# Attention order rewritten: single score tiles with short weighted sums, turns in pairs, row sums for three units at once

## Chip, cores, metric

The kernel runs on one core of one Trainium2 chip. The metric is the device time of one execution in microseconds (us), and the median of several runs is compared. The profile is one further execution, taken by the hardware profiler. PE is TensorE (PEld its weight loads), DVE is VectorE, ACT ScalarE, POOL GpSimd, and SP the engine that issues nearly all DMAs (its queue is shown as SPq).

## The reference, cut

```python
# attention with a learned relative bias, B, H, S, D = 8, 8, 576, 64
scores = (1 / sqrt(D)) * q @ k.T
psi_rel = log1p(abs(i - j)); psi_i = log1p(max(i, 1))
bias = relu((psi_rel / psi_i)[..., None] @ w1 + b1) @ w2       # one value per head
attn = softmax(scores + bias)
x = (attn @ v).transpose(0, 2, 1, 3).reshape(B * S, H * D)     # 4608 x 512
# gated experts' shape, without a nonlinearity; d_ff = 1024
h = (x @ moe_w1) * (x @ moe_w2) @ moe_w3
return h @ moe_w_out
```

## The kernel before

It has three stages. A prologue computes the bias of all heads and writes it to DRAM. Then comes attention, and after it the expert part, whose weights are narrowed from wide words and split into two parts so that matmuls can run in a faster format; `moe_w3` is first multiplied with `moe_w_out` ("fold"), then each block of 512 tokens goes through `up` (L566) and `down` (L592).

Attention goes over 32 **units**. A unit is a pair of heads `p` (4) and a batch entry `b` (8), with `p` outermost, and has nine **tiles** of 128 rows of scores by 576 columns: tiles 0 to 7 hold 128 query rows of one head each (odd ones the second head), tile M the last 64 rows of both heads. The letters below are the names of the steps:

- `lk`, `lq`, `lv`, `c0`, `xd`, `rd`: DMAs on SP. `lk` and `lq` load k and q of a unit (576 KB each, two buffers), `lv` loads v four times, once for each 32 partitions (288 KB each, two buffers), `xd` stores the weighted sums `x`, `rd` the reciprocal row sums in twelve small stores, `c0` loads a piece of an expert weight.
- `S` (L233) on PE: the scores of one tile, four matmuls in 64x64 shape, into one of two PSUM buffers. The trace shows each of these four-byte matmuls as two matmuls with a weight load each, so 8 a tile.
- `T` (L248) on DVE: adds the bias, scales, and takes the row extreme; this frees the PSUM buffer.
- `E` (L270) on ACT: the exponential, with the row sum accumulated into a column of `SUMS`.
- `R` (L280) on DVE: turns the tile in blocks of 32x32 (`nc.vector.transpose`) into `PT`, of which there are two.
- `r` (L283) on DVE: adds a small constant to nine row sums, takes reciprocals and turns them; then `rd`.
- `W` (L301) on PE: the weighted sums, in 32x64 shape, over 18 blocks of 32 keys. Each block is 16 matmuls in the trace, so a unit has 288. Before, they come in four parts of 5, 4, 5 and 4 blocks, that is 80, 64, 80 and 64 matmuls. The first needs the turns of all nine tiles, and the PSUM tile `acc` has one buffer.
- `X` (L318) on ACT: copies `acc` to `x`.
- `c1` to `c7`: a piece of an expert weight is narrowed on the side in 24 of the 32 units, with two steps on ACT, a clamp (L134) and two last steps (L151, L152) on POOL and three steps on DVE (L137, L143, L148).

The order on PE, ACT, DVE and POOL is written out by hand. `arrange` (L38) gives each step a planned time within a unit, in us from the unit's start, and an engine; `drive` (L157) sorts all steps by that time and issues them in that order, so the times decide only which step stands before which on its engine. What an engine really waits for are the semaphores of the tiles. SP takes its DMAs in the same order. A later DMA on SP waits behind an earlier one that can't be issued yet. Each DMA also uses one of eight completion semaphores in turn, and waits for the DMA that used the same one before it.

In the middle of a unit PE's order before is, with the units' distance behind the point:

```
PE  S0 W3(-2) S1 S2 S3 W0(-1) S4 S5 W1(-1) S6 S7 W2(-1) SM | S0 W3(-1) ...
DVE R7(-1) c6 T1 r(-1) RM(-1) T2 R0 T3 R1 T4 R2 T5 R3 T6 R4 T7 R5 c4 TM R6 c5 | T0 ...
SP  lk(+1) lq(+1) c0 lv xd(-2) rd(-1)
```

The weights `w1` and `w2` of the experts are narrowed after attention by the same function `narrow` (L110), in `split_w` (L483).

Of the kernel before, what the change touches and what calls it, by code (L numbers as in the profile page):

```python
# [34 lines left out]
PART_AT = 12, 14, 16, 18


def arrange(NU, pieces):  # L38
# [18 lines left out]
    at["c1"] = 5 * L_T + 2.5, "ACT"  # L57
    at["c2"] = 6 * L_T + 2.5, "ACT"
    at["c3"] = 6 * L_T + 2.0, "POOL"
    for n in range(3):  # L60
        at[f"c{4 + n}"] = (7 + n) * L_T + 2.0, "DVE"
    at["c7"] = 9 * L_T + 3.0, "POOL"
    return {(n, u): (u * PERIOD + t + 1.1, e) for u in range(NU) for n, (t, e) in at.items() if n[0] != "c" or u in pieces}


@with_exitstack
def relpos_attention_moe(
# [39 lines left out]
    LEAST = struct.unpack("<f", struct.pack("<I", 0x38000000))[0]  # L107
    MOST = struct.unpack("<f", struct.pack("<I", 0x47EFFFFF))[0]

    def narrow(pool, src, n, x, queue, pieces=1):  # L110

        d = {}

# [17 lines left out]
            nc.scalar.activation(x, d["lo"].bitcast(U32), AF.Copy, scale=2.0 ** -52)  # L131

        def clamp():
            nc.gpsimd.tensor_scalar(d["mag"], d["mag"], LEAST, MOST, op0=ALU.max, op1=ALU.min)  # L134

        def shift():
            nc.vector.tensor_scalar(  # L137
# [140 lines left out]
    SLOT = {t: 4 if t == "M" else int(t) // 2 + 5 * (int(t) % 2) for t in TILES}

    def op_R(u, t):  # L280
        nc.vector.transpose(PT[u % 2][:, SLOT[t]], st[u].pop(("p", t)))  # L281

    def op_r(u, n):  # L283
        p, b = units[u]
        d = st[u]
        if n == "":
            r = SUMS[u % 3]
            nc.vector.tensor_scalar(r[:, 0:9], r[:, 0:9], 1e-9, None, op0=ALU.add)
            nc.vector.reciprocal(r[:, 0:9], r[:, 0:9])
            d["rt"] = sm.tile([P, 32], F32, name="rt")  # L290
            nc.vector.transpose(d["rt"], r)
            return
        rows = r_d[p][:, b * S:(b + 1) * S]
        for a in range(4):
            for h in range(2):
                o = rows[h, 0:512].rearrange("(i a j) -> a i j", a=4, j=32)[a]
                nc.sync.dma_start(o, d["rt"][32 * a + 4 * h:32 * a + 4 * h + 4])
# [1 line left out]
            nc.sync.dma_start(rows[h:h + 1, j:j + 32], d["rt"][32 * a + 8:32 * a + 9])
# [405 lines left out]
```

## Time and profile before

| | us |
|---|---|
| runs: median (lowest, highest) of 3 | 1337.45 (1331.56, 1342.58) |
| profiled execution: its time | 1344.74 |
| profiled execution: span | 1342.9 |
| first score turn `T` of unit 0 starts | 63.3 |
| last `T` of unit 31 starts | 662.6 |
| expert part, bound by PE, from | 805 |

PE is busy 1147.8 us of the span, DVE 709.0, ACT 495.2, POOL 213.8. The page divides the span into 40 slices of 33.6 us: slices 3 to 20 are attention. A row of a timeline has the start, the duration, the engine, the line, the operation, what is written and read, and in brackets how long the engine was idle before it and what ended the wait; "issue" means that nothing in the profile explains it. In tables of windows each engine has its busy time with the number of instructions, and behind them stand the granted clock of TensorE (1.00 is full), the share of time in which DMA engines were busy, and GB/s.

### The profile page before, as it was taken

To read this page: it belongs to the slowest core of one execution; us is meant where nothing else is said; L and a number is where in the kernel's file an instruction comes from. 1 tells how busy PE (TensorE), PEld (TensorE's weight loads), DVE (VectorE), ACT (ScalarE), POOL (GpSimd) and SP (SyncE) were. 2 spreads that over 40 slices of the span, in tenths; PEclk is the share of its full clock that TensorE was granted. 3 is DMA by queue.
4 is the path that set the end of the run, shared out by engine and by line. 5 is a ranking of instruction groups with operands and counts; after the bars stand their busy time and mean duration, and the time that the engine had idled before them with its cause. 6 is when DMAs were issued, how large, how long until landed. Compare 5 with 4: busy or idle time off the path is not lost. (4 is left out here: it accounts for less than half of the span.)

```text
span 1342.9 us, 34477 instructions
## 1 busy us (share of the span) xinstructions
PE 1147.8 (85%) x14720; PEld 825.3 (61%) x14720; DVE 709.0 (53%) x1468; ACT 495.2 (37%) x1071; POOL 213.8 (16%) x169
## 2 busy tenths in 40 slices
PE   8677777776777768767788999999999999999998
PEld 3244444443544444444576868888888888888887
DVE  8597777767787776687757452222222222222211
ACT  6665545444455444454543332121212121212121
POOL 0012210212012220122256660000000000000000
PEclk9888878888888888788889999999999999999999
DMA  8955567556666567566343221110111110200000
GB/s 255 289 154 165 166 181 218 155 152 176 208 186 170 159 195 198 145 185 172 101 127 125 94 79 59 36 64 32 63 32 63 32 63 32 70 25 32 0 32 32
DMA packets 61497, 158.51 MB, mean 118 GB/s; under 512 B 10400, under 2 KB 18720, under 8 KB 57248
## 3 DMA queue, kind: packets, MB, share of 16 engines
q1 hardware_dynamic: 60912, 156.30, 39.6%
q8 instruction: 115, 1.88, 0.6%
q14 instruction: 38, 0.31, 0.1%
q10 hardware_dynamic: 432, 0.02, 0.0%
HBM read 126.36 MB, written 29.92 MB: 116 GB/s over the span
## 5 line engine op out<-in xcount | busy, mean ns | idle before, releaser
L313 PE MATMUL acc<-pt,v 32*64 32x160 f32 (+1 forms) x9216 | 247.7, 338 | 109.1 <-issue 97.9
L275 ACT ACTIVATE pp<-ts,mx 128x576 f32<-128x576 f32 x288 | 223.1, 775 | 289.5 <-DVE mx L254 285.3
L313 PEld LDWEIGHTS acc<-pt,v 32*64 32x64 f32 x9216 | 195.9, 154 | 184.1 <-issue 166.6
L243 PE MATMUL s<-k,q 64*64 64x288 f32 x2304 | 217.4, 480 | 56.4 <-DVE mx L254 39.0
L254 DVE CUSTOM_DVE_ANT_0 ts<-s,nb 128x576 f32<-128x576 f32 x256 | 186.6, 729 | 78.1 <-PE s L243 63.9
L583 DVE TENSOR_TENSOR g<-up,a 128x512 f32<-128x512 f32 x72 | 49.8, 691 | 337.2 <-PE up L575 337.2
L575 PE MATMUL up<-xh,wl 128*128 128x512 f32 x576 | 225.9, 392 | 2.1 <-DVE wl L494 2.1
L575 PE MATMUL up<-xh,wh 128*128 128x512 f32 x576 | 225.8, 392 | 0.2 <-ACT wh L491 0.2
L575 PE MATMUL up<-xl,wh 128*128 128x512 f32 x576 | 225.6, 392 | 0.0
L281 DVE STREAM_TRANSPOSE pt<-pp 128x576 f32<-128x576 f32 x288 | 221.5, 769 | 0.3 <-ACT pp L275 0.3
L600 PE MATMUL o<-w3s,gh 128*128 128x512 f32 x576 | 178.0, 390 | 0.1
L243 PEld LDWEIGHTS s<-k,q 64*64 64x64 f32 x2304 | 78.2, 150 | 156.9 <-DVE mx L254 85.3
L134 POOL TENSOR_SCALAR wmag<-wmag 128x512 f32<-128x512 f32 x40 | 78.7, 1969 | 355.5 <-ACT wmag L128 354.9
L580 ACT COPY a<-up 128x512 f32<-128x512 f32 x72 | 42.2, 586 | 249.5 <-PE up L575 249.5
L575 PEld LDWEIGHTS up<-xh,wl 128*128 128x128 f32 x576 | 108.3, 188 | 26.7 <-DVE wl L494 3.4
L575 PEld LDWEIGHTS up<-xh,wh 128*128 128x128 f32 x576 | 108.5, 188 | 24.4 <-ACT wh L491 1.0
L575 PEld LDWEIGHTS up<-xl,wh 128*128 128x128 f32 x576 | 108.5, 188 | 23.4
L600 PEld LDWEIGHTS o<-w3s,gh 128*128 128x128 f32 x576 | 108.0, 188 | 23.5 <-ACT gh L586 0.8
L586 ACT ACTIVATE gh<-g 128x512 fp32r<-128x512 f32 x72 | 45.5, 632 | 184.3 <-DVE g L583 184.3
L600 PE MATMUL o<-w3s,gl 128*128 128x512 f32 x288 | 112.3, 390 | 0.9 <-DVE gl L589 0.9
L561 POOL TENSOR_SCALAR xh<-xr 128x512 fp32r<-128x512 f32 x36 | 23.5, 652 | 437.1 <-DVE xr L557 430.4
L589 DVE TENSOR_TENSOR gl<-g,gh 128x512 fp32r<-128x512 f32 x72 | 50.8, 705 | 51.5 <-ACT gh L586 51.5
(63 smaller groups left out, 906.2 us busy)
## 6 DMA issues: line engine op xcount, KB each, us to landing
v<-in_v_dram SPq DMA_DIRECT2D x128, 288.0 KB
k<-in_k_dram SPq DMA_DIRECT2D x32, 576.0 KB
q<-in_q_dram SPq DMA_DIRECT2D x32, 576.0 KB
wi<-in_moe_w_dram SPq DMA_DIRECT2D x32, 512.0 KB
nb_d<-bev SPq DMA_DIRECT2D x36, 295.5 KB
nb<-nb_d SPq DMA_DIRECT2D x16, 576.0 KB
x_d<-x SPq DMA_DIRECT2D x32, 288.0 KB
xr<-x_d SPq DMA_DIRECT2D x36, 256.0 KB
```

The lines of the kernel that those rows point to most:

```text
L134: nc.gpsimd.tensor_scalar(d["mag"], d["mag"], LEAST, MOST, op0=ALU.max, op1=ALU.min)
L243: nc.tensor.matmul(s[outs, hf, :HS], d["q"][rows, h * S + q0:h * S + q0 + 64], d["k"][rows, h * S + hf * HS:h * S + (hf + 1) * HS], start= ...
L254: nc.vector.tensor_tensor_reduce(out=halves(ts), in0=d.pop(("s", t))[:, :, :HS], in1=halves(NB[p, t]), op0=ALU.add, op1=ALU.min, scale=-1. ...
L275: nc.scalar.activation(pp, ts, AF.Exp, bias=mx, scale=-1.0, accum_out=SUMS[u % 3][:, col:col + 1])
L281: nc.vector.transpose(PT[u % 2][:, SLOT[t]], st[u].pop(("p", t)))
L313: nc.tensor.matmul(acc[outs, a, c0:c0 + 32 * (t1 - t0)], x[rows, (h * NBK + b) * D:(h * NBK + b + 1) * D], pt_[rows, t0:t1, 32 * b:32 * b ...
L575: nc.tensor.matmul(acc, l[:, cc], r, start=(n == 0), stop=(n == 3 * NC - 1))
L580: nc.scalar.copy(a, ps[0])
L583: nc.vector.tensor_tensor(g, ps[1], a, op=ALU.mult)
L586: nc.scalar.activation(gh, g, AF.Copy)
L589: nc.vector.tensor_tensor(gl, g, f(gh), op=ALU.subtract)
L600: nc.tensor.matmul(d["o", t], l[:, sl], folded[ft][:, r], start=(ft == 0 and n == 0), stop=(ft == NF - 1 and n == 2),)
```

## The change

The order of attention is written anew, in four ways.

- The tiles are taken as 0 2, 1 3, 4 6, 5 7, M. The exponentials of a pair go to two halves of one tile of 1152 columns, and one `R` turns both (M alone). There are three buffers for a pair and one for M where four held a tile each.
- The weighted sums are in eight parts of 3, 2, 2, 2, 3, 2, 2, 2 blocks, that is 48 or 32 matmuls, and each stands behind a single score tile.
- `r` finishes 27 row sums after every third unit; its `rd` then has 36 stores, and 24 after the last two units.
- The buffers of the pieces (`cva`) become two. `narrow` does its clamp on DVE, except for the pieces within attention, which name POOL as before.

By the new times the order in the middle of a unit is:

```
PE  S0 W6(-2) S2 W7(-2) S1 S3 W0(-1) S4 W1(-1) S6 W2(-1) S5 W3(-1) S7 W4(-1) SM W5(-1) | S0 W6(-1) ...
DVE T0 T2 r(-1) RM(-1) T1 T3 R02 T4 T6 R13 c4 T5 T7 R46 c5 TM R57 c6 | T0 ...
SP  lk(+1) lq(+1) c0 lv xd(-2) rd(-1, every third unit)
```

```diff
-L_T = 1.39
+L_T = 1.43
 PERIOD = 9 * L_T
-TILES = "01234567M"
-NPP, NTS = 4, 3
-PARTS = ((0, 5), (5, 9), (9, 14), (14, 18))
-PART_AT = 12, 14, 16, 18
+TILES = "02134657M"
+PAIRS = ("02", "13", "46", "57", "M")
+NPP, NTS = 3, 3
+PARTS = ((0, 3), (3, 5), (5, 7), (7, 9), (9, 12), (12, 14), (14, 16), (16, 18))
...
 def arrange(NU, pieces):
...
     for k, t in enumerate(TILES):
-        a = k * L_T
-        at["S" + t] = a - 1.1, "PE"
-        at["T" + t] = a + 0.9, "DVE"
-        at["E" + t] = a + 1.7, "ACT"
-        at["R" + t] = a + 2 * L_T + 1.6, "DVE"
-    at["r"] = 10 * L_T + 1.55, "DVE"
-    at["rd"] = 10 * L_T + 2.5, "SP"
-    for n, k in enumerate(PART_AT):
-        at[f"W{n}"] = k * L_T - 0.6, "PE"
+        t_of[k] = (k - k % 2) * L_T + 2.0 + 0.66 * (k % 2)
+        at["T" + t] = t_of[k], "DVE"
+        at["E" + t] = t_of[k] + 0.75, "ACT"
+    s_of = {}
+    for k, t in enumerate(TILES):
+        s_of[k] = t_of[k - 2] + 0.7 if k > 1 else t_of[7 + k] - PERIOD + 0.7
+        at["S" + t] = s_of[k], "PE"
+    for n, ts in enumerate(PAIRS[:-1]):
+        at["R" + ts] = (t_of[2 * n + 2] + (1.33 if n < 3 else 0.67)), "DVE"
+    at["RM"] = PERIOD + t_of[0] + 1.33, "DVE"
+    at["r"] = PERIOD + t_of[0] + 1.30, "DVE"
+    at["rd"] = PERIOD + t_of[0] + 2.5, "SP"
+    for n in range(len(PARTS)):
+        u, k = divmod(n + 3, 9)
+        at[f"W{n}"] = (u + 1) * PERIOD + s_of[k] + 0.3, "PE"
...
-    def narrow(pool, src, n, x, queue, pieces=1):
+    def narrow(pool, src, n, x, queue, pieces=1, clamps=nc.vector):
...
-            nc.gpsimd.tensor_scalar(d["mag"], d["mag"], LEAST, MOST, op0=ALU.max, op1=ALU.min)
+            clamps.tensor_scalar(d["mag"], d["mag"], LEAST, MOST, op0=ALU.max, op1=ALU.min)
...
-    cva = ctx.enter_context(tc.tile_pool(name="cva", bufs=1))
+    cva = ctx.enter_context(tc.tile_pool(name="cva", bufs=2))
...
     def op_E(u, t):
         d = st[u]
         ts, mx = d.pop(("t", t))
-        pp = d["p", t] = ppool.tile([P, S], F32, name="pp", bufs=NPP)
-        col = 8 if t == "M" else int(t) // 2 + 4 * (int(t) % 2)
-        nc.scalar.activation(pp, ts, AF.Exp, bias=mx, scale=-1.0, accum_out=SUMS[u % 3][:, col:col + 1])
+        ps = PAIR[t]
+        if ("p", ps) not in d:
+            if t == "M":
+                d["p", ps] = ppool.tile([P, S], F32, name="ppM")
+            else:
+                d["p", ps] = ppool.tile([P, 2 * S], F32, name="pp", bufs=NPP)
+        k = ps.index(t)
+        col = 9 * (u % 3) + (8 if t == "M" else int(t) // 2 + 4 * (int(t) % 2))
+        nc.scalar.activation(
+            d["p", ps][:, k * S:(k + 1) * S], ts, AF.Exp, bias=mx, scale=-1.0,
+            accum_out=SUMS[u // 3 % 2][:, col:col + 1],
+        )
...
-    def op_R(u, t):
-        nc.vector.transpose(PT[u % 2][:, SLOT[t]], st[u].pop(("p", t)))
+    def op_R(u, ts):
+        s0 = SLOT[ts[0]]
+        o = PT[u % 2][:, s0:s0 + len(ts)].rearrange("p t j -> p (t j)")
+        nc.vector.transpose(o, st[u].pop(("p", ts)))
...
     def op_r(u, n):
+        if u % 3 < 2 and u < NU - 1:
+            return
+        if n == "":
+            r = SUMS[u // 3 % 2]
+            nc.vector.tensor_scalar(r[:, 0:27], r[:, 0:27], 1e-9, None, op0=ALU.add)
+            nc.vector.reciprocal(r[:, 0:27], r[:, 0:27])
+            st[u]["rt"] = sm.tile([P, 32], F32, name="rt")
+            nc.vector.transpose(st[u]["rt"], r)
+            return
+        for w in range(u // 3 * 3, u + 1):
+            sums_out(w, st[u]["rt"][:], 9 * (w % 3))
```

More of the change, by code (lines that the diff above doesn't have):

```diff
@@ L27 @@
 AT_W = 3.5, 0.0, 0.5, 1.2, 2.6, 3.8, 5.5, 7.1, 10.0, 10.6
-L_T = 1.39
+L_T = 1.43
 PERIOD = 9 * L_T
-TILES = "01234567M"
-NPP, NTS = 4, 3
-PARTS = ((0, 5), (5, 9), (9, 14), (14, 18))
-PART_AT = 12, 14, 16, 18
+TILES = "02134657M"
+PAIRS = ("02", "13", "46", "57", "M")
+NPP, NTS = 3, 3
+PARTS = ((0, 3), (3, 5), (5, 7), (7, 9), (9, 12), (12, 14), (14, 16), (16, 18))
 def arrange(NU, pieces):
     at = {}
+    t_of = {}
     for k, t in enumerate(TILES):
-        a = k * L_T
-        at["S" + t] = a - 1.1, "PE"
-        at["T" + t] = a + 0.9, "DVE"
-        at["E" + t] = a + 1.7, "ACT"
-        at["R" + t] = a + 2 * L_T + 1.6, "DVE"
-    at["r"] = 10 * L_T + 1.55, "DVE"
-    at["rd"] = 10 * L_T + 2.5, "SP"
-    for n, k in enumerate(PART_AT):
-        at[f"W{n}"] = k * L_T - 0.6, "PE"
-    at["X"] = PART_AT[-1] * L_T + 1.5, "ACT"
+        t_of[k] = (k - k % 2) * L_T + 2.0 + 0.66 * (k % 2)
[13 more added lines that the diff above has]
+        at[f"W{n}"] = (u + 1) * PERIOD + s_of[k] + 0.3, "PE"
+    at["X"] = at["W7"][0] + 0.9, "ACT"
     at["xd"] = at["X"][0] + 0.8, "SP"
@@ L56, in arrange @@
     at["c0"] = 0.2, "SP"
[L57 to L63, printed above, removed]
+    at["c1"] = t_of[1] + 1.6, "ACT"
+    at["c2"] = t_of[3] + 1.6, "ACT"
+    at["c3"] = t_of[2] + 1.0, "POOL"
+    at["c4"] = t_of[4] + 1.34, "DVE"
+    at["c5"] = t_of[6] + 1.34, "DVE"
+    at["c6"] = t_of[8] + 0.68, "DVE"
+    at["c7"] = t_of[8] + 2.0, "POOL"
+    return {(n, u): (u * PERIOD + t + 1.4, e) for u in range(NU) for n, (t, e) in at.items() if n[0] != "c" or u in pieces}
 @with_exitstack
@@ L264, in relpos_attention_moe @@
     SUMS = []
-    for i in range(3):
+    for i in range(2):
         t = att.enter_context(tc.tile_pool(name=f"sums{i}", bufs=1)).tile([P, 32], F32, name=f"sums{i}")
@@ L268, in relpos_attention_moe @@
         SUMS.append(t)
+    PAIR = {t: ts for ts in PAIRS for t in ts}
     def op_E(u, t):
@@ L272, in op_E, with sums_out @@
         ts, mx = d.pop(("t", t))
-        pp = d["p", t] = ppool.tile([P, S], F32, name="pp", bufs=NPP)
-        col = 8 if t == "M" else int(t) // 2 + 4 * (int(t) % 2)
-        nc.scalar.activation(pp, ts, AF.Exp, bias=mx, scale=-1.0, accum_out=SUMS[u % 3][:, col:col + 1])
+        ps = PAIR[t]
[10 more added lines that the diff above has]
+        )
     SLOT = {t: 4 if t == "M" else int(t) // 2 + 5 * (int(t) % 2) for t in TILES}
-    def op_R(u, t):
-        nc.vector.transpose(PT[u % 2][:, SLOT[t]], st[u].pop(("p", t)))
+    def op_R(u, ts):
+        s0 = SLOT[ts[0]]
+        o = PT[u % 2][:, s0:s0 + len(ts)].rearrange("p t j -> p (t j)")
+        nc.vector.transpose(o, st[u].pop(("p", ts)))
     def op_r(u, n):
-        p, b = units[u]
[L285 to L292, printed above, removed]
+        if u % 3 < 2 and u < NU - 1:
[9 more added lines that the diff above has]
+            sums_out(w, st[u]["rt"][:], 9 * (w % 3))
+    def sums_out(u, rt, c0):
+        p, b = units[u]
         rows = r_d[p][:, b * S:(b + 1) * S]
@@ L296, in op_r @@
                 o = rows[h, 0:512].rearrange("(i a j) -> a i j", a=4, j=32)[a]
-                nc.sync.dma_start(o, d["rt"][32 * a + 4 * h:32 * a + 4 * h + 4])
+                nc.sync.dma_start(o, rt[32 * a + c0 + 4 * h:32 * a + c0 + 4 * h + 4])
             h, j = a // 2, 512 + a % 2 * 32
-            nc.sync.dma_start(rows[h:h + 1, j:j + 32], d["rt"][32 * a + 8:32 * a + 9])
+            nc.sync.dma_start(rows[h:h + 1, j:j + 32], rt[32 * a + c0 + 8:32 * a + c0 + 9])
     def op_W(u, n):
@@ L337, in piece_of @@
         if i < NF:
-            return narrow(cva, moe_w_out[i * P:(i + 1) * P, :], DO, wos[i], nc.sync)
+            return narrow(cva, moe_w_out[i * P:(i + 1) * P, :], DO, wos[i], nc.sync, clamps=nc.gpsimd)
         ft, hf = divmod(i - NF, 2)
         cs = slice(hf * 512, (hf + 1) * 512)
-        return narrow(cva, moe_w3[ft * P:(ft + 1) * P, cs], 512, w3s[ft][:, cs], nc.sync)
+        return narrow(cva, moe_w3[ft * P:(ft + 1) * P, cs], 512, w3s[ft][:, cs], nc.sync, clamps=nc.gpsimd)
     pieces = dict(zip([u for u in range(NU) if 0 < u % B < B - 1], (piece_of(i) for i in range(3 * NF))))
```

## The prediction

> **What bounds the kernel now.** I read the windows first, then the timeline of TensorE over one unit, then VectorE, the weight loads and the DMA issues. The window from the first score turn (`op_T`) of unit 3 to the first one of unit 31 holds 28 units; columns are PE, PEld, DVE, ACT, POOL busy with counts, then granted clock, DMA share, GB/s.
>
> ```profile
> 107.12:647.67 540.55, 394.05 (x10084) 240.53 (x10080) 401.06 (x907) 265.12 (x633) 97.98 (x66) 0.85 0.63 176
> ```
>
> 540.55 / 28 = **19.3 us a unit**. PE is busy 14.1 of it, DVE 14.3: no engine is full, so the unit is set by waits. TensorE over a little more than one unit (start, duration, engine, idle before it and its releaser):
>
> ```profile
> 312.88 0.50 PE L313 MATMUL acc<-pt,v 32*64 32x128 f32 x9 [3.18 <-issue]
> 313.31 1.48 PE L243 MATMUL s<-k,q 64*64 64x288 f32 x16
> 314.72 2.94 PE L313 MATMUL acc<-pt,v 32*64 32x160 f32 x80
> 317.59 1.20 PE L243 MATMUL s<-k,q 64*64 64x288 f32 x16
> 318.72 1.37 PE L313 MATMUL acc<-pt,v 32*64 32x160 f32 x64
> 320.02 0.72 PE L243 MATMUL s<-k,q 64*64 64x288 f32 x8
> 321.14 0.71 PE L243 MATMUL s<-k,q 64*64 64x288 f32 x8 [0.41 <-DVE mx L254]
> 322.82 0.71 PE L243 MATMUL s<-k,q 64*64 64x288 f32 x8 [0.96 <-DVE mx L254]
> 324.90 2.98 PE L313 MATMUL acc<-pt,v 32*64 32x160 f32 x80 [1.37 <-issue]
> 327.81 1.20 PE L243 MATMUL s<-k,q 64*64 64x288 f32 x16
> 328.94 1.37 PE L313 MATMUL acc<-pt,v 32*64 32x160 f32 x64
> 330.23 1.23 PE L243 MATMUL s<-k,q 64*64 64x288 f32 x14
> 334.53 1.11 PE L243 MATMUL s<-k,q 64*64 64x288 f32 x2 [3.07 <-issue]
> ```
>
> Twice PE stops for over 3 us in the middle of a run of matmuls that wait for no tile ("issue"), the second time inside one score part (14 + 2). Between the two stops stand 9+16+80+16+64+8+8+8+80+16+64+14 = 383 matmuls. The page says what comes in lumps of that kind:
>
> ```profile
> PE 1147.8 (85%) x14720; PEld 825.3 (61%) x14720; DVE 709.0 (53%) x1468; ACT 495.2 (37%) x1071; POOL 213.8 (16%) x169
> ...
> q8 instruction: 115, 1.88, 0.6%
> ...
> v<-in_v_dram SPq DMA_DIRECT2D x128, 288.0 KB
> ```
>
> 1.88 MB in 115 packets is 16 KB each; 2 x 14720 PE instructions over 115 packets are 256 each, so 128 matmuls with their weight loads, and 383 is three such blocks. I read the stop as **a late block of instructions**. Why it is late stands in the DMA issues:
>
> ```profile
> 323.95 1.76 SPq L227 DMA_DIRECT2D v<-in_v_dram  x4
> ...
> 326.34 0.90 SPq L297 DMA_DIRECT2D r_d<-rt  x2
> ...
> 335.70 0.59 SPq L297 DMA_DIRECT2D r_d<-rt  x2
> 336.33 0.25 SPq L299 DMA_DIRECT2D r_d<-rt  x1
> 339.03 0.36 SPq L230 DMA_DIRECT2D k<-in_k_dram  x1
> ```
>
> The stretch that ends in the stop begins 128 matmuls earlier, about 326.6 (34 before the end of the run of 324.90), when the next block can first be asked for; then v (four loads of 288 KB) is in the queues, and at the 176 GB/s of the window it alone takes 6.7 us. Asked for at 326.6, at work at 334.53: 7.9 us, and the block in hand lasted to 331.46. The two block ends between the stops show no stop. The stop costs a second time:
>
> ```profile
> 331.19:334.60 3.41, 0.34 (x7) 0.07 (x1) 1.55 (x4) 2.37 (x6) 1.92 (x1) 1.00 0.35 101
> 334.60:338.01 3.41, 3.41 (x79) 2.55 (x81) 1.76 (x4) 0.87 (x2) 0.00 (x0) 0.50 0.02 6
> ```
>
> After 3.4 us with PE busy 0.34 the clock is granted at 0.50 for the next 3.4 us, and 80 matmuls take 2.94 us where, by the slope of 64 in 1.37 at full clock, they would take about 1.65. [...]
>
> **VectorE.** Its dense cadence, the row sums and the narrowing steps:
>
> ```profile
> 300.56 0.65 DVE L143 SCALAR_TENSOR_TENSOR wmag<-wi,wmag 128x512 int32<-128x512 int32 x1
> ...
> 302.50 0.39 DVE L148 TENSOR_SCALAR wi<-wmag 128x512 int32<-128x512 int32 x1
> ...
> 303.48 0.84 DVE L288 TENSOR_SCALAR sums<-sums 128x9 f32<-128x9 f32 x1
> ...
> 304.74 0.21 DVE L291 STREAM_TRANSPOSE rt<-sums 128x32 f32<-128x32 f32 x1 [0.16 <-DVE sums L289]
> 304.87 0.73 DVE L281 STREAM_TRANSPOSE pt<-pp 128x576 f32<-128x576 f32 x1
> 305.53 0.72 DVE L254 CUSTOM_DVE_ANT_0 ts<-s,nb 128x576 f32<-128x576 f32 x1
> ...
> 306.88 0.72 DVE L254 CUSTOM_DVE_ANT_0 ts<-s,nb 128x576 f32<-128x576 f32 x1
> ...
> 314.09 0.76 DVE L254 CUSTOM_DVE_ANT_0 ts<-s,nb 128x576 f32<-128x576 f32 x1 [3.09 <-PE s L243]
> ...
> 316.82 0.38 DVE L137 TENSOR_SCALAR wmag<-wmag 128x512 int32<-128x512 int32 x1
> ```
>
> T to T with one turn between is 306.88 - 305.53 = 1.35 us: 0.66 for T, 0.69 for the turn. So a unit needs 9 x 1.35 = 12.15, plus row sums 304.87 - 303.48 = 1.39, plus narrowing 0.65 + 0.39 + 0.38 = 1.42 where there is a piece: 15.0 us. The rest to 19.3 is waiting for scores (3.09 here), that is for PE and its late code.
>
> **The change, part by part.** *Pairs of turns.* A turn of 576 columns shows 0.73, one of 32 columns 0.21: (0.73 - 0.21) / 544 = 0.96 ns a column, so 1152 columns add 0.55 to a turn's 0.69: 1.24 against 1.38 for two. No such turn is in the trace; the bounds are 1.38 (no gain) and 1.10 (576 more columns at 0.72 of that slope). I take 1.27. Two T in a row cost what one T and a half-turn slot show, 0.69:
>
> ```profile
> 63.34 0.76 DVE L254 CUSTOM_DVE_ANT_0 ts<-s,nb 128x576 f32<-128x576 f32 x1 [11.11 <-DMA nb_d<-bev]
> ...
> 64.03 0.75 DVE L254 CUSTOM_DVE_ANT_0 ts<-s,nb 128x576 f32<-128x576 f32 x1
> ```
>
> A pair is then 0.69 + 0.66 + 1.27 = 2.62, a unit 4 x 2.62 + 1.35 = 11.8. *Row sums once in three units:* 1.39 / 3 = 0.46; the 18 further columns are under 0.02. They also stop holding RM: today RM follows the sums and the first weighted sum needs RM, the 1.37 of wait at 324.90; this goes in two units of three. DVE: 11.8 + 0.46 + 1.42 = **13.7** with a piece (24 units), 12.3 without (8).
>
> *Eight parts behind single score tiles.* This costs PE, since it changes between the two shapes eight times a unit each way, not four:
>
> ```profile
> 298.40 0.69 PEld L243 LDWEIGHTS s<-k,q 64*64 64x64 f32 x16 [0.23 <-issue]
> 299.53 1.07 PEld L313 LDWEIGHTS acc<-pt,v 32*64 32x64 f32 x64 [0.44 <-issue]
> 300.82 0.21 PEld L243 LDWEIGHTS s<-k,q 64*64 64x64 f32 x8 [0.22 <-DVE pt L281]
> ```
>
> A score tile is 0.69 / 2 = 0.35 and 0.44 of switch; a part is 0.0167 a matmul and 0.23. New unit: seven single tiles 7 x 0.79, one double 1.13, six parts of 32 at 0.76, two of 48 at 1.03: 5.5 + 1.1 + 4.6 + 2.1 = **13.3 us** at full clock. Today: four groups of tiles (2, 2, 2, 3) 4.9 and parts of 80 and 64 twice each, 5.7: 10.6. So 2.7 us of PE a unit are added, and PE becomes as long as DVE. [...]
>
> What is bought with it: today a run of 64 to 80 matmuls sits between two scores while DVE has two score buffers; the new longest run is 48, and a block of code lasts 128 / 360 of a unit, 5.6 us at 15.8, where the one before the stop lasted 331.46 - 326.6 = 4.9. The block that took 7.9 us behind v would stop PE 2.3 us instead of 3.1, one asked for at a random point of the 6.7 us of v about half of that. I take **1.2 us a unit** for the stops (bounds 0 and 3.1), and no half clock, since a window with 1.2 us of stop is still busy over half.
>
> Two engines of 13.3 to 13.7 that take turns through two buffers don't run at their maximum. The nearest rows are the waits of PE for DVE in the stretch without a stop, 0.41 at 321.14 and 0.96 at 322.82, 1.4 a unit: I take 0.9 us (bounds 0 and 1.4). Sum: 13.7 + 0.9 + 1.2 = **15.8 us a unit**, against 19.3.
>
> *The DMA issues.* The twelve small r_d stores a unit become 36 behind one x_d of every third unit. SP issues in order and the next k, q, the piece and v stand behind them. Today twelve take from 326.34 to 336.58, but the first eight wait for v; the last three go at 0.3 us each (335.70 to 336.58). So from the issue of v to the last store 12.6 us become 12.6 + 24 x 0.3 = 19.8, and SP is free about 22 us after the k load that opened the unit, 6 us after the next one is due. k and q are asked for a whole unit ahead and land in about 5 us, so they have 10 to spare. Of v: k, q, the piece and v are 2.9 MB, 16 us at 176 GB/s; it lands up to 38 us after that first k load, and by the order it is needed 2.3 units after it, at 36: 0 to 2 us late in every third unit, 0 to 0.7 a unit. I cost it at 0, hidden by the unit of lead. *Second wi buffer (`cva` 2):* the load of a piece no longer waits for GpSimd's last step; with it v is issued earlier. Nothing on the path. *The order 02134657M* only follows the bias groups: 0.
>
> *The clamp of the expert weights goes from GpSimd to VectorE* (the stage after attention):
>
> ```profile
> DVE wmag L137 <- POOL wmag L134: 29.9, 11, 4.4
> PE w3t L522 <- DVE w3l L528: 10.7, 8, 4.1
> ```
>
> (waits from 676 to 830 us: total, times, longest). VectorE stands 29.9 us behind GpSimd's clamp, and PE 10.7 behind VectorE. Sixteen clamps on DVE at about 0.38, the size of L137, add 6.1 us to an engine that then has 29.9 less of waiting. I take 6 of the 10.7 us as gained (bounds 0 and 14 with the half clocks that follow). From 805 us on nothing changes.
>
> **Sum.** 28 x (19.3 - 15.8) = 98 us, 2 for unit 2, 6 for the weights: 106 off the profiled execution, whose span is 1342.9 us and whose time is 1344.74. The median of the runs is 1337.45, 7.3 below it, so **1232 us**.
>
> **Rivals.** *A, the stops vanish* and only the coupling of DVE and PE is left: 14.6 us a unit, 28 x 4.7 + 8 = 140 off, 1197. For it: blocks last longer; against: v still lies in the way in each unit. *B, the stops stay whole.* If they have a cause other than late code, or if k, q, the piece and v, now issued back to back, hold the fetch more often, 3.3 us a unit remain (half clock with it): 13.7 + 0.9 + 3.3 = 17.9, 28 x 1.4 + 6 = 45 off, 1292. For it: the same stop twice in the rows above, one unit apart. [...] *C, slower: the burst of 36 r_d stores.* If they go at the pace of all twelve today, 10.2 / 12 = 0.85 us, they take 31 us and end 37 us after the k load; v lands 12 later at 49, 13 late in each third unit: 4.4 a unit, 20.2, so 28 x 0.9 = 25 lost, 8 gained, 1354. It costs from about 0.35 us a store and turns into a loss near 0.7. Against it: 0.3 at the end of the row. *D, no change:* the unit is bound by something that I don't see: 1335.
>
> **How the numbers follow.** Forecast 0.48, A 0.20, B 0.22, C 0.06, D 0.04. The range takes in A and B with the bounds of their terms (coupling 0 in A: 1172; SP's 0.7 a unit in B: 1312), cut to about two in ten left out: 1180 to 1300. About 1% is what a measurement of this kernel tells from no change (the runs spread from 1331.56 to 1342.58). Faster 0.89, same 0.05, slower 0.06.
>
> **What the profile of after would show.** First scores of units about 15.8 us apart; turns of 128x1152 near 1.3 us; PE busy over eight tenths of the stage with a clock over 0.93; "issue" waits of PE under 2 us each; r_d stores at 0.3 us; no wait of VectorE for L134 after 676 us. I would be wrong if stops of 3 us stand in each unit, if PE waits for v, or if the parts' switch costs more than 0.67 us each way and back.

## The result, and the profile after

The changed kernel takes **1269.54 us** (median of 4 runs, 1264.82 to 1275.14) where the kernel before takes 1334.51 (4 runs, 1330.94 to 1342.58): a ratio of **0.951** (95% interval 0.944 to 0.957). The forecast of 1232 was 37 us too fast, inside the range of 1180 to 1300, and the measured time lies nearer to rival B (1292), though not for B's reason, as the experiments show. The page of the profiled execution after (time 1275.14 us, span 1273.4 us):

```profile
q8 instruction: 115, 1.88, 0.6%
```

The amount of code is what it was, 115 packets. The windows after, with the columns as before: the stage from the first `T` of unit 3 to that of unit 31, and then units 11 to 14, each from its first `T` to that of the next unit.

```profile
110.34:590.69 480.35, 397.38 (x10138) 208.32 (x10120) 377.52 (x741) 255.89 (x632) 98.20 (x66) 0.89 0.68 197
...
241.60:263.10 21.50, 19.34 (x432) 10.24 (x430) 13.68 (x27) 9.30 (x23) 3.84 (x3) 0.76 0.78 230
263.10:279.97 16.87, 13.99 (x353) 7.05 (x348) 13.96 (x30) 9.65 (x23) 4.47 (x3) 0.90 0.56 155
279.97:293.41 13.44, 11.17 (x321) 5.73 (x311) 13.19 (x27) 9.21 (x23) 4.47 (x3) 1.00 0.63 176
293.41:315.82 22.41, 17.84 (x395) 9.44 (x399) 13.65 (x27) 9.44 (x23) 4.45 (x3) 0.70 0.67 195
```

480.35 / 28 = **17.2 us a unit**, against 19.3 before and 15.8 forecast. The units are not alike. Unit 13 takes 13.44 us, with VectorE busy 13.19 and the full clock: nearly the forecast's bound for VectorE. Units 11 and 14 take over 21, with the clock at 0.76 and 0.70. These long units stand three apart, as the bursts of row sums do: over the stage the nine units 5, 8, 11 to 29 average 19.5 us, the other nineteen 16.0. The trace's clock rows show 1.00 or 0.50 and nothing else, so a mean of c over a stage means half clock for 2 x (1 - c) of it: 2 x 0.11 x 480 = 106 us here, and 2 x 0.15 x 541 = 162 before.

What SP issues around units 12 to 14 (timeline of its queue):

```profile
259.93 0.35 SPq L238 DMA_DIRECT2D k<-in_k_dram  x1
...
265.26 0.61 SPq L322 DMA_DIRECT2D r_d<-rt  x2
...
279.20 0.25 SPq L324 DMA_DIRECT2D r_d<-rt  x1
279.50 0.59 SPq L322 DMA_DIRECT2D r_d<-rt  x2
280.13 0.25 SPq L324 DMA_DIRECT2D r_d<-rt  x1
...
283.85 0.25 SPq L324 DMA_DIRECT2D r_d<-rt  x1
284.20 0.36 SPq L238 DMA_DIRECT2D k<-in_k_dram  x1
...
289.93 0.35 SPq L238 DMA_DIRECT2D k<-in_k_dram  x1
```

The 36 stores run from 265.26 to 284.1. Once v is out of the way (its last packet ends at 274.4) they go at 0.31 us each (three from 279.20 to 280.13), and SP is free 24 us after the k load of 259.93: close to the 0.3 and the 22 of the forecast. What the forecast did not follow is what comes next. The k load of 284.20 is so late that the following one, 289.93, comes 6 us behind it, and the loads of two units, two pieces included, go out together. In windows, first during the stores and then behind them:

```profile
276.40:284.10 7.70, 7.31 (x204) 3.64 (x206) 7.70 (x16) 4.66 (x13) 2.73 (x3) 1.00 0.03 5
285.30:307.30 22.00, 17.48 (x436) 9.18 (x432) 16.60 (x34) 12.28 (x31) 4.99 (x4) 0.84 0.98 286
```

The DMA engines are empty for 7.7 us (share 0.03) and then full for 22 us (0.98, 286 GB/s). What that does shows in two ways. The first is at the burst before, around the start of unit 11 (its first `T` is at 241.60), in the timelines of SP, PE and ACT:

```profile
232.17 0.25 SPq L324 DMA_DIRECT2D r_d<-rt  x1
232.52 0.36 SPq L238 DMA_DIRECT2D k<-in_k_dram  x1
232.92 1.20 SPq L238 DMA_DIRECT2D q<-in_q_dram  x1
```

```profile
240.82 0.71 PE L251 MATMUL s<-k,q 64*64 64x288 f32 x8 [3.01 <-DMA q<-in_q_dram]
```

```profile
253.78 0.66 ACT L136 ACTIVATE wmag<-wi 128x512 f32<-128x512 f32 x1 [5.68 <-DMA wi<-in_moe_w_dram]
```

k and q of the unit are asked for only when the stores are out, 9.1 us before its first `T`; before the change the k load of 339.03 came 20.0 us ahead of its unit's (359.0). q lands after 7.9 us, and TensorE has waited 3.01 us for it. The piece lands later still, and ScalarE, whose next exponentials stand behind it, waits 5.68 us.

The second is late code. In the 22 us from 285.30 TensorE stops twice (its timeline):

```profile
291.18 0.34 PE L338 MATMUL acc<-pt,v 32*64 32x160 f32 x1
294.02 1.37 PE L338 MATMUL acc<-pt,v 32*64 32x160 f32 x31 [2.50 <-issue]
...
309.24 1.24 PE L251 MATMUL s<-k,q 64*64 64x288 f32 x8 [3.96 <-issue]
```

No tile is waited for ("issue"), and the first stop falls inside a part (1 + 31), as the late code of before did. The trace's DMA packets show the code itself: a packet of the instruction queue runs from 291.05 to 292.29 and another from 306.65 to 307.77, and TensorE goes on 1.7 and 1.5 us later. All 19 "issue" waits of over 0.8 us in the stage end 1.2 to 1.8 us after such a packet. A stop can cost a second time. Two pairs of windows, around the first of these stops and around an earlier, shorter one (1.45 us, until 271.39):

```profile
290.01:293.42 3.41, 1.51 (x41) 0.63 (x29) 3.41 (x7) 1.25 (x4) 0.00 (x0) 1.00 0.97 224
293.42:296.83 3.41, 2.81 (x53) 1.51 (x61) 0.95 (x4) 0.00 (x0) 2.53 (x2) 0.50 0.97 373
...
269.53:272.94 3.41, 1.96 (x66) 1.00 (x50) 2.60 (x5) 1.48 (x4) 0.00 (x0) 1.00 0.93 217
272.94:276.35 3.41, 3.41 (x76) 1.72 (x58) 1.63 (x5) 1.27 (x3) 0.00 (x0) 0.50 0.25 78
```

After 3.41 us with PE busy 1.51 (0.44) or even 1.96 (0.57), the next 3.41 us are granted at 0.50. The windows are 3.41 us long because every half-clock row of the trace in this stage lasts 3.41 us or twice that. No run shows a sharp threshold: the window from 112.51, busy 0.53, was followed by full clock, that from 563.07, busy 0.63, by half.

### The profile page after: what moved, and what is told of

It reads as the page before. It is cut to its first block, busy times and chain, and to the rows that moved or that the text cites. A ratio compares the mean times of both kernels' runs of the same rounds, so it can differ in the third digit from the quotient of the medians.

```text
span 1273.4 us, 34086 instructions
## 1 busy us (share of the span) xinstructions
PE 1149.2 (90%) x14720; PEld 789.4 (62%) x14720; DVE 695.9 (55%) x1293; ACT 485.7 (38%) x1071; POOL 181.1 (14%) x152
## 4 chain that ended last, share of the span: by engine, by line
PE 68%; DMA 12%; DVE 7%; issue 5%; SPq 3%; ACT 3%; POOL 0%; DVEq 0%; ACTq 0%; POOLq 0%
PE up L600 31%; PE o L625 15%; PE acc L338 10%; PE s L251 9%; DMA wi<-in_moe_w_dram 3%; PE wacc L559 3%; DVE ts L262 2%; DVE pt L301 2%; DMA q<-in_q_dram 2%; DMA x_d<-x 2%; DMA nb_d<-bev 2%; SPq L322 2%; DMA nb<-nb_d 1%; ACT pp L291 1%; DMA wi<-in_moe_w_out_dram 1%
## 5 line engine op out<-in xcount | busy, mean ns | idle before, releaser
L338 PE MATMUL acc<-pt,v 32*64 32x160 f32 (+1 forms) x9216 | 260.0, 319 | 48.3 <-issue 37.3
L338 PEld LDWEIGHTS acc<-pt,v 32*64 32x64 f32 x9216 | 170.8, 143 | 180.9 <-issue 153.0
L251 PE MATMUL s<-k,q 64*64 64x288 f32 x2304 | 228.2, 471 | 53.5 <-DVE mx L262 24.2
L262 DVE CUSTOM_DVE_ANT_0 ts<-s,nb 128x576 f32<-128x576 f32 x256 | 186.9, 746 | 110.3 <-PE s L251 68.5
L291 ACT ACTIVATE pp<-ts,mx 128x576 f32<-128x576 f32 x256 | 196.4, 769 | 82.4 <-DVE mx L262 80.5
L301 DVE STREAM_TRANSPOSE pt<-pp 128x1152 f32<-128x1152 f32 x128 | 175.9, 1374 | 0.0
L251 PEld LDWEIGHTS s<-k,q 64*64 64x64 f32 x2304 | 68.8, 144 | 137.5 <-issue 56.0
L142 POOL TENSOR_SCALAR wmag<-wmag 128x512 f32<-128x512 f32 x24 | 46.0, 1917 | 272.0 <-ACT wmag L136 264.3
```

What stands on the lines that cost most here:

```text
L142: clamps.tensor_scalar(d["mag"], d["mag"], LEAST, MOST, op0=ALU.max, op1=ALU.min)
L251: nc.tensor.matmul(s[outs, hf, :HS], d["q"][rows, h * S + q0:h * S + q0 + 64], d["k"][rows, h * S + hf * HS:h * S + (hf + 1) * HS], start= ...
L262: nc.vector.tensor_tensor_reduce(out=halves(ts), in0=d.pop(("s", t))[:, :, :HS], in1=halves(NB[p, t]), op0=ALU.add, op1=ALU.min, scale=-1. ...
L291: nc.scalar.activation(d["p", ps][:, k * S:(k + 1) * S], ts, AF.Exp, bias=mx, scale=-1.0, accum_out=SUMS[u // 3 % 2][:, col:col + 1],)
L301: nc.vector.transpose(o, st[u].pop(("p", ts)))
L338: nc.tensor.matmul(acc[outs, a, c0:c0 + 32 * (t1 - t0)], x[rows, (h * NBK + b) * D:(h * NBK + b + 1) * D], pt_[rows, t0:t1, 32 * b:32 * b ...
```

## The experiments

Two theories stood after the result. **Burst:** the 36 stores push two units' loads together, and late code in that bunch makes the missing 1.4 us a unit. **Stops anyway:** late code behind v was priced too low, wherever the stores stand. A unit's time is always the stage from the first `T` of unit 3 to that of unit 31, divided by 28. Ratios are to the kernel before, run beside each.

**Spread the stores.** The 36 stores of three units go out in three of twelve, one in each of the following units; the row sums are still finished once in three.

```diff
...
-        for w in range(u // 3 * 3, u + 1):
+        for w in range(max(0, u - 2), u + 1 if last else u - 1):
             sums_out(w, st[w]["rt"][:], 9 * (w % 3))
```

> The changed kernel, but the row sums' stores go out as 12 behind each unit (still finished on VectorE once for three units), not as 36 behind every third. Theory 1, the burst: in the changed kernel's trace every third unit takes about 20.6 us and the others about 15.0; the 36 stores hold SP for some 8 us while the DMA engines stand idle, the loads of two units then come together, code comes late and the clock halves. Spread, the third units should come down to 15 to 16 us: 10 x 5 = 50 us less, 1220 us (1205 to 1240). Rival 2, volume: the long units come from the DMA volume and where the code blocks fall; then nothing changes, 1265 (1255 to 1280). Rival 3: twelve stores in each unit hold SP a little in all of them, as before the change, and what is won in one unit is lost in the other two: 1250 to 1265 without a pattern of three.

Measured: 1249.39 us, ratio 0.932 (0.927 to 0.937).

```profile
112.60:564.50 451.90, 386.41 (x10100) 202.33 (x10103) 375.80 (x742) 255.53 (x632) 98.15 (x66) 0.92 0.74 209
```

451.90 / 28 = 16.1 us a unit, 1.0 below the changed kernel: that is what the burst costs. Through what, the waits over the stage show (total, times, longest), first of the changed kernel and then of this one:

```profile
PE acc L338 <- issue: 31.4, 22, 4.0
PE s L251 <- DMA q<-in_q_dram: 13.2, 4, 4.2
PE s L251 <- issue: 10.6, 7, 4.0
...
ACT wmag L136 <- DMA wi<-in_moe_w_dram: 12.8, 4, 5.7
ACT wmag L136 <- DMA wi<-in_moe_w_out_dram: 5.3, 1, 5.3
```

```profile
PE acc L341 <- issue: 40.2, 27, 4.5
PE s L251 <- issue: 9.8, 7, 2.6
PE acc L341 <- DMA q<-in_q_dram: 0.2, 1, 0.2
```

Late loads go: TensorE's waits for q fall from 13.2 us to 0.2, and ScalarE's 18.1 us for the pieces are not there any more. Late code does not go: the "issue" waits are 31.4 + 10.6 = 42.0 us in the changed kernel and 40.2 + 9.8 = 50.0 here. Of the 28 us of the stage (480.35 - 451.90) 17.5 are idle time of TensorE (13.0 less for q, 8.0 more for late code, the rest other waits), and 11.0 are busy time (397.38 - 386.41), which goes with the clock, 0.89 and 0.92. So the first theory has the right place, but its late code is not what the burst adds. The unit is still 0.3 above the forecast, and 1.8 us a unit of late code are left, as the second theory says.

**Finish the row sums in each unit,** with twelve stores a unit, in the otherwise new order.

```diff
-        if u % 3 < 2 and u < NU - 1:
-            return
...
-            r = SUMS[u // 3 % 2]
-            nc.vector.tensor_scalar(r[:, 0:27], r[:, 0:27], 1e-9, None, op0=ALU.add)
-            nc.vector.reciprocal(r[:, 0:27], r[:, 0:27])
+            r = SUMS[u % 3]
+            nc.vector.tensor_scalar(r[:, 0:9], r[:, 0:9], 1e-9, None, op0=ALU.add)
+            nc.vector.reciprocal(r[:, 0:9], r[:, 0:9])
...
-        for w in range(u // 3 * 3, u + 1):
-            sums_out(w, st[u]["rt"][:], 9 * (w % 3))
+        sums_out(u, st[u]["rt"][:], 0)
```

> The changed kernel with the row sums finished and stored in each unit, as before the change. VectorE pays 0.9 us more a unit (1.39 each against 0.46), and the first weighted sum waits again for the turn of tile M behind the sums. Theory 1, the burst: no unit is long any more (15.0 + 0.9 + some 0.5 of wait, 16.4 against a mean of 17.2 now): 28 x 0.8 = 22 us less, 1245 (1230 to 1258). Rival 2, volume: the batch is a gain without a price, and undoing it costs 28 x 1.2 = 34 us: 1300 (1285 to 1315). Rival 3: about as the first experiment plus 25.

Measured: 1257.95 us, 0.938 (0.934 to 0.943).

```profile
105.80:578.60 472.80, 389.12 (x10091) 204.96 (x10080) 383.92 (x795) 256.17 (x632) 98.07 (x66) 0.91 0.71 201
```

16.9 us a unit: 0.75 more than with spread stores and batched row sums, where the rows of before gave 1.39 - 0.46 = 0.93 for the batch, and about 0.3 less than the changed kernel. As it stood, the batch lost a little more through its burst than it saved on VectorE.

**Four parts instead of eight,** as before, in the otherwise new order.

```diff
-PARTS = ((0, 3), (3, 5), (5, 7), (7, 9), (9, 12), (12, 14), (14, 16), (16, 18))
+PARTS = ((0, 5), (5, 9), (9, 14), (14, 18))
...
-        u, k = divmod(n + 3, 9)
+        u, k = divmod(2 * n + 4, 9)
...
```

> The changed kernel with the weighted sums in four parts (80, 64, 80, 64 matmuls) behind every second score tile, not eight. The step of the prediction: eight parts cost TensorE 2.7 us a unit in switches of shape (10.6 against 13.3 us) and buy even use of code and of the two score buffers. If TensorE's length is what bounds the units, four parts are faster: units of 13.7 to 14.5 us where no stop is, 1269 - 28 x 1.0 = 1240. If evenness is what pays, VectorE waits for scores behind 80 matmuls (1.6 us) and code comes late after 3 to 4.5 us of dense work: 28 x 1.0 more, 1297. I expect the second, 1285 (1260 to 1310).

Measured: 1269.20 us, 0.948 (0.942 to 0.954), the changed kernel's own time within the intervals.

```profile
109.30:591.30 482.00, 368.29 (x10132) 218.32 (x10131) 375.69 (x741) 255.15 (x632) 98.19 (x66) 0.90 0.69 195
```

17.2 a unit too. PE is busy 29 us less than in the changed kernel (397.38 - 368.29, 1.0 a unit), and none of it reaches the end. The waits of PE for VectorE (`mx`) rise instead, from 15.2 us to 52.1, and late code costs the same, 42.5 us of "issue". With the burst in place, cutting the weighted sums into eight was worth nothing that can be measured.

**Other queues.** The spread stores issued by ScalarE, and, in a second kernel, v issued by ScalarE in four steps with the spread stores on SP.

```diff
-                nc.sync.dma_start(o, rt[32 * a + c0 + 4 * h:32 * a + c0 + 4 * h + 4])
+                nc.scalar.dma_start(o, rt[32 * a + c0 + 4 * h:32 * a + c0 + 4 * h + 4])
...
```

> As the first experiment (12 stores behind each unit), with these stores issued by ScalarE instead of SP. Theory 1: SP then issues only the loads and x, the loads of a unit are never held, and ScalarE has 12 x 0.3 = 3.6 us a unit more on about 11 of 15: at or under the first experiment, 1210 (1195 to 1235). Rival 2: 1265. Against it: if the stores wait on ScalarE for earlier ones to land, its exponentials come late and VectorE's turns with them: 1290.

```diff
-            for a in range(4):
-                nc.sync.dma_start(t[32 * a:32 * a + 32], v[p, b])
+            nc.scalar.dma_start(t[32 * a:32 * a + 32], v[p, b])
...
+    for a in range(4):
+        at[f"lv{a}"] = 3.8 + 2.1 * a, "ACT"
```

> The first experiment with v's four loads of a unit issued by ScalarE, 2.1 us apart in the planned order, instead of by SP in one go. Same bytes. Theory 1: a block of code now waits for one quarter of v at most (1.3 us), so stops and half clocks mostly go: 40 us under the first experiment, 1208 (1190 to 1230). Rival 2: the bytes count, not their grouping: 1249 (1240 to 1258). Rival 3: ScalarE waits at a load as it did at the stores in e4: 1270 or more.

Measured: stores on ScalarE 1327.39 us, 0.992 (0.989 to 0.995); v on ScalarE 1290.47, 0.965 (0.961 to 0.969). Both lose to the spread stores. ScalarE's largest wait behind a DMA over the stage, of the one and of the other:

```profile
ACT pp L291 <- DMA r_d<-rt: 171.1, 28, 11.5
```

```profile
ACT pp L293 <- DMA r_d<-rt: 68.3, 21, 6.4
```

ScalarE has to make the exponentials, and it stands 171.1 and 68.3 us in waits that the profile puts down to row-sum stores. In the second kernel it issues none of them. In the first, the issuing itself is a good part of it, twelve stores of some 0.3 us a unit. The semaphores in the trace say what else it waits for: there are eight, taken in turn by the DMAs of SP and of ScalarE (in the stage of the changed kernel, where SP issues all of them, each serves 72 or 73 of 580 DMAs, and 451 of these wait for the one that they use), so a DMA on ScalarE waits for an older one that holds its own, and the exponentials wait behind it. In the first kernel these older ones are mostly SP's loads. Its stores of 297.43, 299.85 and 301.20 go out just when q, the piece and the first quarter of v have landed, and the next exponential, at 303.15, has waited 5.51 us. In the second kernel they are SP's stores.

**Leave v's loads out.** v of units 0 and 1 is used again in all later units, in the kernel before and in the one with spread stores.

```diff
-        if which == "v":
+        if which == "v" and u > 1:
+            t = st[u - 2]["v"]
+        elif which == "v":
```

> The kernel before, with v loaded for units 0 and 1 only; all later units use these two again (their weighted sums are of the wrong v; all other work is there). Theory 1, late code behind v: the stop of TensorE of 3.5 us a unit goes, and the half clock behind it (164 us of half clock in the 28 units). What is left is VectorE's own 15.0 us and some 0.4: 28 x 3.9 = 109 us less than before, 1230 (1215 to 1250). Rival: the stops have another cause than v in the queues; then 1325 to 1340, the stops in the trace as before.

> The first experiment (stores spread, 12 a unit) with v loaded for units 0 and 1 only, as in e5. Theory 1: without v ahead of it code comes in time in 5 us blocks; the unit is then VectorE's 13.7 and TensorE's 13.3 with what their coupling costs, by the prediction 14.6 and by the shortest units seen (13.44) less: 14.0 x 28, so 60 us under the first experiment, 1189 (1175 to 1210). Rival: k, q and the piece hold the code as much as v, or the clock halves for other reasons: 1220 to 1245.

Measured, with two runs each: before without v 1261.96 us, 0.943 (0.938 to 0.948); spread without v 1184.64, 0.885 (0.881 to 0.890).

```profile
107.30:564.10 456.80, 375.10 (x10080) 231.83 (x10080) 402.10 (x908) 266.07 (x633) 97.86 (x66) 0.84 0.42 136
```

```profile
106.60:505.00 398.40, 359.55 (x10090) 188.66 (x10080) 370.81 (x741) 257.46 (x632) 98.38 (x66) 0.98 0.47 154
```

Before, v costs 19.3 - 16.3 = 3.0 us a unit; in the new order with spread stores 16.1 - 14.2 = 1.9. The "issue" waits of PE fall from 110.8 us to 5.4 before (of the 110.8 some 29 do not follow a packet of code and are other waits, such as the 1.37 of the prediction's rows), and from 50.0 to 14.3 with spread stores: most of the late code comes with v's loads. Without v the new order is worth 16.3 - 14.2 = 2.1 a unit and runs at a clock of 0.98. The kernel before, without v, is the surprise: its stops all but go, yet its clock stays at 0.84. Its timeline and two windows show why:

```profile
306.93 0.77 PE L245 MATMUL s<-k,q 64*64 64x288 f32 x8 [0.96 <-DVE mx L256]
309.06 2.97 PE L315 MATMUL acc<-pt,v 32*64 32x160 f32 x80 [1.36 <-DVE pt L283]
```

```profile
304.05:307.46 3.41, 1.62 (x24) 0.42 (x16) 3.41 (x8) 2.45 (x8) 1.13 (x1) 1.00 0.74 293
307.46:310.87 3.41, 2.05 (x64) 1.84 (x64) 3.22 (x10) 1.24 (x4) 1.41 (x2) 0.50 0.62 156
```

Single scores and a first weighted sum that wait for VectorE leave PE busy 1.62 of 3.41 us, and the clock halves with no late code in that stretch. The new order keeps PE busy there. I take the short weighted sums between the scores to be what does it, but no run without v has the new order with four parts, so that is not shown.

**The clamp back on POOL,** for the weights after attention, in the otherwise new kernel.

```diff
-    def narrow(pool, src, n, x, queue, pieces=1, clamps=nc.vector):
+    def narrow(pool, src, n, x, queue, pieces=1, clamps=nc.gpsimd):
```

> The changed kernel with the clamps of the expert weights back on GpSimd (in attention they are there anyway). The prediction put the move at 6 us (0 to 14): 1269 + 6 = 1275 (1269 to 1283). Rival: TensorE's waits after attention come from elsewhere, and it is worth nothing: 1269. Attention's units are untouched by it.

Measured: 1287.65 us, 0.962 (0.958 to 0.965). The wait of this kernel after attention that is gone from the changed one:

```profile
DVE wmag L145 <- POOL wmag L142: 31.7, 12, 4.4
```

The last `T` of attention starts at 601.08 in the changed kernel and at 596.75 in this one. From there to the end it is 1273.4 - 601.1 = 672.3 us and 1281.3 (this kernel's span) - 596.75 = 684.6: the clamp on VectorE is worth 12 us, by one profiled execution of each; the medians of the runs lie 18 apart.

**Turns one at a time,** two for each pair, in the otherwise new kernel.

```diff
-        nc.vector.transpose(o, st[u].pop(("p", ts)))
+        pp = st[u].pop(("p", ts))
+        for k in range(len(ts)):
+            nc.vector.transpose(PT[u % 2][:, s0 + k], pp[:, k * S:(k + 1) * S])
```

> The changed kernel with each pair turned by two instructions of 576 columns, not one of 1152. The prediction gave a pair of turns 0.11 us of gain over two single ones, 0.44 us a unit, if VectorE bounds the unit: 28 x 0.44 = 12 us slower at most, 1278 (1268 to 1284). Rival: stops and the burst set the units, and VectorE has that much to spare: 1269.

Measured: 1272.41 us, 0.953 (0.948 to 0.958): no difference that can be told. VectorE's timeline, of the changed kernel and then of this one:

```profile
278.37 1.37 DVE L301 STREAM_TRANSPOSE pt<-pp 128x1152 f32<-128x1152 f32 x1
279.67 0.39 DVE L156 TENSOR_SCALAR wi<-wmag 128x512 int32<-128x512 int32 x1
```

```profile
248.29 1.43 DVE L302 STREAM_TRANSPOSE pt<-pp 128x576 f32<-128x576 f32 x2
249.65 0.72 DVE L262 CUSTOM_DVE_ANT_0 ts<-s,nb 128x576 f32<-128x576 f32 x1
```

From the start of a turn to the next instruction a pair takes 1.30 us (279.67 - 278.37) and two singles 1.36: 0.06 a pair, 0.2 a unit, where 0.11 a pair had been forecast.

**v in one DMA instead of four.** One load whose source is read four times over (the outermost dimension has step 0), with spread stores and in the kernel before.

```diff
-            for a in range(4):
-                nc.sync.dma_start(t[32 * a:32 * a + 32], v[p, b])
+            src = v[p, b]
+            src = bass.AP(tensor=src.tensor, offset=src.offset, ap=[[0, 4]] + list(src.ap))
+            nc.sync.dma_start(t, src)
```

> The first experiment (stores spread) with v loaded by one DMA into all 128 partitions (the source read four times) where four DMAs wrote 32 partitions each; the bytes are the same, 1152 KB. Theory 1: what makes code late is the time that v's packets stand in the queues. In the traces v's rows take about 0.64 us per 9.2 KB, k and q, which go to 128 partitions, 0.18 us per 4.6 KB. If one DMA over 128 partitions runs as k and q do, v's 6 us become about 3, the stops of 1.9 us a unit (16.1 against 14.2 without v) about 0.8: 28 x 1.1 = 31 us under the first experiment, 1218 (1200 to 1235). Rival: the bytes count, however they are written: 1249 (1240 to 1258).

> The kernel before with v in one DMA, as in e9. Without v it took 3.0 us a unit less (16.3 against 19.3). Theory 1: with v half as long in the queues half of that goes, 28 x 1.5 = 42 us: 1296 (1275 to 1315). Rival: no change, 1338.

Measured: 1545.49 us, 1.158 (1.151 to 1.164), and 1599.04, 1.200 (1.192 to 1.208). Both fall far on the slow side, for a reason of their own. The first kernel's window while v is on its way:

```profile
301.40:325.10 23.70, 14.75 (x398) 8.21 (x405) 13.99 (x29) 10.52 (x27) 4.73 (x4) 0.78 0.25 94
```

A share of 0.25 is what four of the 16 engines give when they are always busy; k and q, alone in the queues of the kernel before, held 0.97 (281.5 to 283.5), and the four loads of v 0.99 (287.5 to 292.5). All that moves, the end of an older load with it, goes at 94 GB/s. The load of v issued at 300.70 writes its last row at 323.9, some 23 us later, and in the 500 us from 150 TensorE waits 164.6 us for v itself. Four is also the number of repeats; that the one follows from the other is my guess, no other count was run. The runs say nothing on queued loads and late code.

**v in one DMA over 128 partitions,** with v laid out four times in DRAM, and spread stores.

```diff
-            for a in range(4):
-                nc.sync.dma_start(t[32 * a:32 * a + 32], v[p, b])
+            nc.sync.dma_start(t, v[p, b])
...
```

> The first experiment with v given in four copies in DRAM, as q and k are given in two, so that one DMA of 128 rows of 9.2 KB loads it over all 16 engines; 1152 KB a unit as before. (The single DMA of e9 repeated v in its outermost dimension of 4 and moved 108 KB a us from 300 to 323 us, as four engines would, each row in 0.35 us; with all 16 writing the same 32 partitions a row takes 0.64.) Theory 1, the time of v in the queues: at 0.35 a row v takes 8 x 0.35 = 2.8 us in place of 5 to 6, and of the 1.9 us a unit that v costs (16.1 against 14.2 without it) 1.0 goes: 28 us under the first experiment, 1221 (1200 to 1236). Rival: the bytes count and not the time they stand in the queues: 1249 (1240 to 1258).

Measured: 1243.83 us, 0.932 (0.927 to 0.936), the spread kernel's 0.932 again.

```profile
115.50:565.30 449.80, 382.86 (x10128) 199.77 (x10120) 375.83 (x742) 256.78 (x632) 98.29 (x66) 0.94 0.61 210
```

The DMA engines' time of the stage fell from 0.74 x 451.9 = 334 us to 0.61 x 449.8 = 274. v's own packets (9.2 KB each, 3584 in either stage) fell from 145 us of all 16 engines to 98, that is from 5.2 us a unit to 3.5, and the unit from 16.1 to 16.1. The "issue" waits of PE did fall, from 50.0 us to 40.7, but its idle time as a whole did not (65.5 and 66.9 us): other waits took their place. So the time that v holds the engines sets at most a part of late code, and shortening it gained nothing. What else of v does it, its bytes, its place in the order or its 128 rows, **stays open**.

## Why the prediction was right and wrong

**What bounds the kernel: right in kind.** Without v's loads the stops all but go and a unit of before falls by 3.0 us. That the stops are late code is shown by the packets of the instruction queue that end 1.2 to 1.8 us before PE goes on (so all 19 stops of over 0.8 us after; before, for the stop until 334.53, a packet from 331.79 to 333.10); that a block is 128 matmuls, by the expert part of before, where the sixteen packets from 876.9 to 1314.6 stand 125 to 132 matmuls apart; that v's loads bring them, by their removal ("issue" waits of 110.8 us against 5.4, and of 50.0 against 14.3); by which of v's properties they hold the code is open (above). But "the stop costs a second time" could not be priced from the rows of before: with hardly a stop its clock stayed at 0.84, and there the half clock came behind single scores that waited for VectorE. What it cost before was not measured by itself.

**VectorE, 13.7 a unit: right.** Unit 13, which finishes no row sums, runs at 13.44, dense, where 13.7 - 0.46 = 13.24 stood. Pairs of turns gave less (1.30 for 1.27 each). **The coupling of 0.9 was right:** without v the unit is 14.2, where 13.7 + 0.9 = 14.6 stood. The sum took 13.7 for every unit, though by its own count six of these 28 have no piece and need 12.3; their mean is 13.4, and the coupling that was measured is then 0.8.

**The switches, 13.3 of PE a unit: too dear.** Between 276.4 and 293.4 a single score and a part of 32 follow each other like this (timeline of PE after):

```profile
280.79 1.40 PE L251 MATMUL s<-k,q 64*64 64x288 f32 x16 [0.21 <-DVE mx L262]
282.36 1.07 PE L338 MATMUL acc<-pt,v 32*64 32x160 f32 x48 [0.17 <-PE s L251]
283.36 0.71 PE L251 MATMUL s<-k,q 64*64 64x288 f32 x8
284.01 0.80 PE L338 MATMUL acc<-pt,v 32*64 32x160 f32 x32
284.74 0.71 PE L251 MATMUL s<-k,q 64*64 64x288 f32 x8
```

A score takes 0.65 from start to start (0.79 forecast), a part of 32 0.73 (0.76), one of 48 1.00 (1.03). With a double score of 1.4 (1.13 forecast), a unit is 7 x 0.65 + 1.4 + 6 x 0.73 + 2 x 1.00 = 12.3 us. The kernel with four parts agrees: there PE is busy 1.0 a unit less, where the working had 2.7. The spare time of PE was worth little, since none of that 1.0 reached the end.

**The burst, costed at 0 (bounds 0 to 0.7): the step that failed.** It measured **1.0 us a unit, 28 us in all**. The working asked the right question, whether k, q and v land before they are needed, and had the pace of the stores (0.31) and SP's 24 us nearly right. It failed at the step "k and q are asked for a whole unit ahead and land in about 5 us, so they have 10 to spare". Behind a burst the k load of unit 11 came 25.4 us after the one before it (232.52 - 207.09), in a unit of 14.4 us: 11 late, not 6. q then took 7.9 us to land, not 5, and nothing was left over. TensorE waited 13.2 us for q, and ScalarE 18.1 for the pieces, whose way behind the stores the working did not follow; v, for which it allowed up to 0.7, was never waited for. Rival C had the place and the kind right, loads that land late behind the stores, but the wrong load (v) and the wrong pace (0.85 a store). Rival B's "now issued back to back, hold the fetch more often" is not what happened: the "issue" waits of PE are 42.0 us with the burst and 50.0 without. That the time lies nearer to B than to the forecast is chance.

**The stops, 1.2 a unit (bounds 0 to 3.1): nearly right. "No half clock": wrong.** The "issue" waits of the stage are 42.0 us, 1.5 a unit, and 1.8 with the stores spread; before they were 2.9, counting those that follow a packet of code (81.4 us). What shortened them is open, since four parts have 1.5 too. But a stop was priced as the mean of a unit. It comes as 29 stops, eight of them of 2.0 to 4.0 us, and such a stop can leave its window busy for less than half, as at 291.52 to 294.02 (0.44); and over half was no safety either, since a window with 1.45 us of stop, busy 0.57, was followed by half clock. So the half clock came too: 106 us of it after. Stops and half clock together, with the stores spread, are the 1.9 a unit that v costs: 0.7 x 28 = 20 us more than forecast.

**The sum.** Base and coupling 0.4 below, stops with their half clock 0.7 above, burst 1.0 above: 17.16 instead of 15.8 a unit, 38 us. The stage gave 540.55 - 480.35 = 60.2 us. From the last `T` to the end it is 1342.9 - 662.6 = 680.3 before and 672.3 after, 8.0 gained, of which the clamp alone is worth 12 (forecast 6, bounds 0 to 14); what took 4 back is not shown by itself, but TensorE has a stop of 3.35 us for code there (until 605.21), and before it had none. From the end of the stage to the last `T` 4.5 were gained (662.6 - 647.7 = 14.9, and 601.1 - 590.7 = 10.4), and the first units lost 3.2 (107.1 to 110.3). 60.2 + 8.0 + 4.5 - 3.2 = 69.5 off the span, for 106 forecast. **Second wi buffer and tile order, 0:** not tried alone.

**What the profile of after was to show.** Turns near 1.3: yes (1.30 to the next instruction). Stores at 0.3: yes. The wait for the clamp gone: yes. PE busy over eight tenths: yes, 397.38 of 480.35, but at a clock of 0.89 instead of 0.93. First scores 15.8 apart: no, 17.2. "Issue" waits under 2 us each: no, eight of 29 are longer. Of the three signs of being wrong none came as it stood: there is not a stop of 3 us in each unit, PE never waits for v (but for q), and the switch costs less.

**A better version.** Spread stores alone beat both kernels, at 0.932; with v in one DMA over 128 partitions as well it is the same within the intervals.

## What to carry to other kernels

When a batch of small DMAs is put into one place of an in-order queue, follow every load that stands behind it, and give each the lead that the batch leaves, not the one of before: here 20 us of lead became 9, the load took 7.9 with the next ones on its heels, and the engines that needed q and the piece waited. Batch the arithmetic, but spread its stores. Before calling a bunch of loads the cause of late code, compare the total of such waits with and without the bunch. And look for the half clock behind windows as little busy as those here, up to 0.63 of 3.41 us, whatever made them so: here small waits (0.48) did it as well as one stop (0.44).
